# Rows of experts 2 to 6 turned by transposing transfers instead of by TensorE

## The chip, the cores and the metric

The kernel runs on one core of a Trainium2 chip. The core has five engines with queues of their own: TensorE (PE; PEld is its weight load), VectorE (DVE), ScalarE (ACT), GpSimd (POOL) and SyncE (SP), and 16 DMA engines that move what POOL, SP and ACT issue. The metric is device time in microseconds (us) of one execution, lower is better, given as the median of several runs.

## The reference

A chunked attention with memory (4 batches, 8 heads, 768 positions, head size 64) gives 3072 rows of 512 numbers. A noisy top-2 router sends each row to two of eight experts, and each expert is a two-layer product with a ReLU between:

```python
noisy_logits = logits + noise_scale * noise
top2 = np.argpartition(-noisy_logits, 2, axis=1)[:, :2]
...
for e in range(E):
    for k in range(2):
        mask = top2[:, k] == e
        h = np.maximum(x[mask] @ w1[e], 0.0)
        out[mask] += top2_w[mask, k, None] * (h @ w2[e])
```

Here `w1[e]` is 512 x 1024 and `w2[e]` is 1024 x 512. The change lies in the expert part alone.

## The kernel before

The first part (to about 110 us of the span) computes attention and router, and writes all rows with their eight gates to a table in device memory, `x_rows`. A row is 264 words: 512 bf16 numbers in 256 words, then 8 gates.

The second part works by *buckets*. Each pair of experts (28 pairs) has a bucket of up to 128 rows that chose both. `gather` (L693 to L699) fetches a bucket's rows by an indirect transfer on POOL's queue into one of eight `xl` buffers, row by partition. `turn` (L701 to L707) brings it into the form in which the first product reads it: four TensorE transposes of 128x128 into PSUM, one VectorE copy to the bucket's columns of `xTb`, and one ScalarE copy of the gates into `meta`. Rows over a bucket's limit take a side path (`spill`, `spart`) that the change does not touch.

Experts run one after the other (L877). For expert e, `first` (L758) multiplies `w1[e]` with the `xTb` columns of its seven buckets, in two groups (`big`, four buckets, 512 columns; `small`, three, 384 columns), each in eight `ps_h` groups of four matmuls, with four PSUM buffers; the ReLUs alternate between ScalarE (L754) and VectorE (L756). Then `second` (L777) does one bucket after another: eight matmuls into one of two `ps_y` buffers, drained with the gate as scale by ScalarE into an accumulator (the bucket's first expert) or by VectorE onto it (its second), after which POOL scatters the rows to the output (L788) and SP copies six rows to `spart` (L795).

A bucket is gathered and turned once, for the earlier of its two experts: `plan[e]` holds the new buckets of expert e, 7, 6, 5, 4, 3, 2, 1 and 0 of them. The order is written out by hand. After `first` of expert e the gathers of `plan[e + 1]` are issued, then the load of `w1[e + 2]`; after each bucket of `second` one of `plan[e + 1]` is turned; at the end `w2[e + 2]` is loaded. The weight loads, gathers and scatters are all on POOL's queue, in this order. SP has only the `spart` and `meta` transfers of the side path here.

Of the kernel before, what the change touches and what calls it, by code (L numbers as in the profile page):

```python
# [12 lines left out]
F32 = mybir.dt.float32  # L13
BF16 = mybir.dt.bfloat16
# [10 lines left out]
def kernel(  # L25
# [14 lines left out]
    nc = tc.nc  # L40
# [7 lines left out]
    E, F = moe_w1.shape[0], moe_w1.shape[2]  # L48
    KP = Dm // 128
# [19 lines left out]
    XC = Dm // 2  # L69
# [12 lines left out]
    def color(p):  # L82
        a, d = p % E, p // E + 1
        side = 0 if d == E // 2 else (a >> (1 if d == 2 else 0)) & 1
        return side * (E // 2) + d - 1
# [13 lines left out]
    def body():  # L99
# [63 lines left out]
        for hd in range(2 * GP):  # L163
            nc.sync.dma_start(
                out=mv_nat[QW * hd + WP:QW * hd + QW].rearrange("p g e d -> p g (e d)"),
                in_=bass.AP(mem_v.tensor, mem_v.offset + hd * n_mem * D, [[2 * D, n_mem // 2], [2 * GP * n_mem * D, NG], [1, 2 * D]]))
# [369 lines left out]
        def load_w1(e):  # L536
            w1t = w1bufs[e % 3]
            nc.gpsimd.dma_start(out=w1t, in_=moe_w1[e].rearrange("(kp p) f -> p kp f", p=128))
            W1[e] = w1t

        def load_w2(e):
            w2t = w2bufs[e % 3]
            nc.gpsimd.dma_start(out=w2t, in_=moe_w2[e].rearrange("(fb p) d -> p fb d", p=128))
            W2[e] = w2t
# [140 lines left out]
        xTv = xTb.rearrange("p k (g c) -> p k g c", c=CAP)  # L685
        meta = xg.tile([128, NB, E], F32, name="meta")
# [4 lines left out]
        got = {}  # L691

        def gather(p):  # L693
            idx = gidx if p in plan[0] else gidx2
            xl = ld.tile([128, ROW], I32, name="xl")
            nc.gpsimd.indirect_dma_start(  # L696
                out=xl, out_offset=None, in_=xd, in_offset=bass.IndirectOffsetOnAxis(ap=idx[:, p:p + 1], axis=0),
                bounds_check=N - 1, oob_is_err=True)
            got[p] = xl  # L699

        def turn(p, other=False):  # L701
            xl = got[p]
            p_t = psY.tile([128, KP, CAP], BF16, name="p_t2", tag="ps_y") if other else psX.tile([128, KP, CAP], BF16, name="p_t")
            for kp in range(KP):
                nc.tensor.transpose(out=p_t[:, kp, :], in_=xl[:, kp * 64:(kp + 1) * 64].bitcast(BF16), identity=identb)  # L705
            nc.vector.tensor_copy(xTv[:, :, p, :], p_t)  # L706
            nc.scalar.copy(meta[:, p, :], xl[:, XC:].bitcast(F32))  # L707

        def gather_spill(s_gi):
            xl = ld.tile([128, ROW], I32, name="xl")  # L710
            nc.gpsimd.indirect_dma_start(
                out=xl[:SPILL], out_offset=None, in_=xd, in_offset=bass.IndirectOffsetOnAxis(ap=s_gi[:, 0:1], axis=0),
                bounds_check=N - 1, oob_is_err=True)
            got["s"] = xl
# [17 lines left out]
        def halves(e):  # L732
            up = [(d - 1) * E + e for d in range(1, E // 2 + 1) if d < E // 2 or e < E // 2]
            dn = [(d - 1) * E + (e - d) % E for d in range(1, E // 2 + 1) if d < E // 2 or e >= E // 2]
            return sorted((sorted(up), sorted(dn)), key=lambda x: -len(x))
# [62 lines left out]
        plan = []  # L798
# [78 lines left out]
        for e in range(E):  # L877
            big, small = halves(e)
            if e == E - 1:
                end = nc.values_load(n_spill_i[0:1, 0:1], min_val=SPILL, max_val=N)  # L880
                past = xg.tile([128, NP], F32, name="past")
                nc.vector.tensor_scalar(out=past, in0=srank, scalar1=-float(SPILL), scalar2=None, op0=Alu.add)
            ht = hp_.tile([128, FB, (E - 1) * CAP], BF16, name="ht")
            if e == 0:
                parts = [big[:2], big[2:], small]
                off = 0
                for x, ps in enumerate(parts):
                    for j, p in enumerate(ps):
                        turn(p, j % 2 == 1)
                    if x == 2:  # L890
                        turn_spill()
                        find_tails()
                    first(W1[e], ht, off, ps, nc.scalar if x == 0 else None, CAP if x == 2 else OWN, big if x == 2 else ())
                    off += len(ps)
                    if x == 0:
                        s_gi, s_si = find_spill()
                        gather_spill(s_gi)
                        load_w2(1)
            else:
                first(W1[e], ht, 0, big)  # L900
                first(W1[e], ht, len(big), small)
            nxt = list(plan[e + 1]) if e + 1 < E else []
            for p in nxt:
                gather(p)
            if e + 2 < E:
                load_w1(e + 2)
            order = big + small

            for j, p in enumerate(order):
                second(e, p, ht, j, W2[e])  # L910
                if nxt:
                    turn(nxt.pop(0))
                if e == E - 1 and j == 1:
                    for x in range(1, E // 2 - 1):
                        nc.vector.tensor_tensor(out=spart[:, 0, :], in0=spart[:, 0, :], in1=spart[:, x, :], op=Alu.add)
            if e == E - 1:
                assert color(order[-1]) >= NCOL
                nc.vector.tensor_tensor(out=spart[:, 0, :], in0=spart[:, 0, :], in1=spart[:, E // 2 - 1, :], op=Alu.add)
                nc.gpsimd.indirect_dma_start(
                    out=out_part[NB], out_offset=bass.IndirectOffsetOnAxis(ap=s_si[:, 0:1], axis=0),  # L920
                    in_=spart[:, 0, :], in_offset=None, bounds_check=N - 1, oob_is_err=False)
            while nxt:
                turn(nxt.pop(0))
            if e + 2 < E:
                load_w2(e + 2)
        return end, past, ovc, ramp_i, onesb, identb, psX, psY, first, ld, hp_, xg, accs, load_w1, load_w2, W1, W2, relu, psH

    with tc.manual_schedule():
        kept = body()
# [3 lines left out]
    with tc.For_i(SPILL, end, 128) as i:  # L933
# [7 lines left out]
        for t in range(NP):  # L941
# [11 lines left out]
            out=xl, out_offset=None, in_=xd, in_offset=bass.IndirectOffsetOnAxis(ap=gi[:, 0:1], axis=0),  # L953
# [10 lines left out]
        with tc.For_i(0, E, 1) as e:  # L964
# [17 lines left out]
            out=out, out_offset=bass.IndirectOffsetOnAxis(ap=si[:, 0:1], axis=0),  # L982
            in_=o, in_offset=None, bounds_check=N - 1, oob_is_err=False)
# [30 lines left out]
```

## Time and profile before

| | |
|---|---|
| median of 3 runs | 337.96 us (335.78 to 338.23) |
| the profiled execution | 335.33 us, its span 333.7 us |
| mean granted clock of TensorE | 0.957 |
| TensorE (PE) busy | 288.1 us, 86% |
| DVE, ACT, POOL busy | 169.9, 133.4, 138.6 us |
| first product (L769) | 640 matmuls |
| second product (L780) | 448 matmuls |
| turns (L705) | 112 matmuls, 28 buckets |
| gathers (L696) | 28, median 6.5 us from issue to landing |

The profile is of one execution. A row of a group has line, engine, operation, tiles and shapes, then busy us, mean ns of one, and the idle time ahead of it with what ended it. Times in an order of time are us from the start of the span. Matmuls are pipelined, so the drawn lengths of neighbours overlap, and the distance between starts is what counts. L numbers are those of the kernel before, unless the kernel after is named.

### The profile page before, as it was taken

To read this page: it belongs to the slowest core of one execution; us is meant where nothing else is said; L and a number is where in the kernel's file an instruction comes from. 1 tells how busy PE (TensorE), PEld (TensorE's weight loads), DVE (VectorE), ACT (ScalarE), POOL (GpSimd) and SP (SyncE) were. 2 spreads that over 40 slices of the span, in tenths; PEclk is the share of its full clock that TensorE was granted. 3 is DMA by queue.
4 is the path that set the end of the run, shared out by engine and by line. 5 is a ranking of instruction groups with operands and counts; after the bars stand their busy time and mean duration, and the time that the engine had idled before them with its cause. 6 is when DMAs were issued, how large, how long until landed. Compare 5 with 4: busy or idle time off the path is not lost.

```text
span 333.7 us, 7301 instructions
## 1 busy us (share of the span) xinstructions
PE 288.1 (86%) x3019; PEld 173.5 (52%) x3019; DVE 169.9 (51%) x343; ACT 133.4 (40%) x235; POOL 138.6 (42%) x181
## 2 busy tenths in 40 slices
PE   1697887977776377999999999999999999999990
PEld 0575675755654256554754754544544544544540
DVE  7789859849958775222322323424342433434451
ACT  7877788757433033533333332332303303202200
POOL 7877868538023472781008007007152042042152
PEclk9999999979989559999999999999999999999997
DMA  7999999999997136699407905914959624521031
GB/s 99 179 163 176 184 163 163 210 143 101 214 225 216 23 88 93 128 156 238 87 0 125 221 4 110 223 28 105 207 147 166 117 111 70 86 109 60 1 140 71
DMA packets 58763, 42.99 MB, mean 129 GB/s; under 512 B 32449, under 2 KB 52033, under 8 KB 58728
## 3 DMA queue, kind: packets, MB, share of 16 engines
q0 software_dynamic: 49808, 38.71, 77.0%
q1 hardware_dynamic: 8632, 3.74, 5.6%
q8 instruction: 24, 0.39, 0.5%
q10 hardware_dynamic: 288, 0.07, 0.1%
q14 instruction: 11, 0.09, 0.1%
HBM read 61.23 MB, written 10.66 MB: 215 GB/s over the span
## 4 chain that ended last, share of the span: by engine, by line
PE 43%; issue 24%; DVE 13%; ACT 8%; POOL 7%; DMA 3%; POOLq 0%; DVEq 0%; ACTq 0%
PE ps_h L769 16%; PE ps_y L780 14%; POOL out_dram L788 4%; ACT kd L276 3%; PE ps_o L345 3%; DMA out_dram<-acc,sidx 2%; PE ps_o L341 2%; DVE mx L313 2%; DVE xrow L358 2%; DVE sd L318 2%; DVE vg L150 2%; PE p_t L705 2%; ACT xt L371 1%; ACT P L320 1%; PE p_t L265 1%
## 5 line engine op out<-in xcount | busy, mean ns | idle before, releaser
L769 PE MATMUL ps_h<-xTb,w1t 128*128 128x512 bf16 (+5 forms) x640 | 101.4, 320 | 1.5 <-DVE xTb L706 1.5
L780 PE MATMUL ps_y<-w2t,ht 128*128 128x512 bf16 x448 | 101.4, 379 | 0.0
L769 PEld LDWEIGHTS <-w1t 128*128 128x128 bf16 x640 | 58.6, 99 | 43.9 <-DVE xTb L706 1.1
L788 POOL DMA_INDIRECT out_dram<-acc,sidx x28 | 28.1, 1004 | 126.4 <-DVE acc L787 124.1
L756 DVE TENSOR_SCALAR ht<-ps_h 128x512 bf16<-128x512 f32 (+3 forms) x68 | 38.1, 560 | 68.1 <-PE ps_h L769 63.1
L780 PEld LDWEIGHTS <-ht 128*128 128x128 bf16 x448 | 42.9, 98 | 46.7
L754 ACT ACTIVATE ht<-ps_h 128x384 bf16<-128x384 f32 (+2 forms) x76 | 38.9, 511 | 70.4 <-PE ps_h L769 66.3
L784 ACT ACTIVATE acc<-ps_y,meta 128x512 f32<-128x512 f32 x28 | 19.2, 687 | 62.6 <-PE ps_y L780 45.4
L787 DVE SCALAR_TENSOR_TENSOR acc<-ps_y,meta,acc 128x512 f32<-128x512 f32 x28 | 21.0, 750 | 34.5 <-PE ps_y L780 34.5
L696 POOL DMA_INDIRECT xl<-x_rows,gidx x28 | 30.0, 1071 | 16.8 <-PE ps_h L769 6.6
L134 POOL DMA_DIRECT2D vg<-in_v_dram x34 | 25.5, 756 | 11.4 <-DMA kg<-in_k_dram 3.7
L706 DVE COPY xTb<-p_t 128x512 bf16<-128x512 bf16 x28 | 11.6, 422 | 28.6 <-PE p_t L705 28.4
L276 ACT COPY kd<-p_t 64x768 bf16<-64x768 bf16 x32 | 25.2, 786 | 1.0 <-PE p_t L265 0.8
L265 PE MATMUL p_t<-identb,qg 128*64 128x128 bf16 x192 | 10.3, 245 | 12.0 <-DMA qg<-in_q_dram 6.6
L371 ACT COPY xt<-p_x 128x768 bf16<-128x768 bf16 x16 | 12.8, 798 | 12.0 <-PE p_x L369 11.9
L341 PE MATMUL ps_o<-memv,PT 128*128 128x260 bf16 x96 | 15.0, 296 | 2.2 <-DVE PT L332 2.0
L320 ACT ACTIVATE P<-sd 128x768 bf16<-128x768 f32 x16 | 13.5, 845 | 8.1 <-DVE sd L318 8.1
L268 ACT COPY qT<-p_t 128x768 bf16<-128x768 bf16 x16 | 12.8, 800 | 8.9 <-PE p_t L265 8.8
L358 DVE TENSOR_TENSOR xrow<-ps_o,rec 128x768 bf16<-128x768 f32 x16 | 15.3, 958 | 0.6
L313 DVE TENSOR_REDUCE mx<-ps_s 128x12 f32<-128x768 f32 x16 | 15.1, 942 | 0.5 <-PE ps_s L300 0.5
L318 DVE TENSOR_TENSOR sd<-ps_s,mx 128x768 f32<-128x768 f32 x16 | 15.2, 949 | 0.0
L345 PE MATMUL ps_o<-vg,PT 128*32 128x256 bf16 x384 | 14.9, 293 | 0.0
(150 smaller groups left out, 287.5 us busy)
## 6 DMA issues: line engine op xcount, KB each, us to landing
w1t<-in_moe_w_dram POOLq DMA_DIRECT2D x8, 1024.0 KB, 11.4
w2t<-in_moe_w_dram POOLq DMA_DIRECT2D x8, 1024.0 KB, 10.1
vg<-in_v_dram POOLq DMA_DIRECT2D x30, 168.0 KB, 10.2
qg<-in_q_dram POOLq DMA_DIRECT2D x7, 384.0 KB, 9.9
kg<-in_k_dram POOLq DMA_DIRECT2D x7, 384.0 KB, 11.3
x_rows<-xrow SPq DMA_DIRECT2D x3, 792.0 KB
x_rows<-xrow SPq DMA_DIRECT2D x2, 384.0 KB
xl<-x_rows,gidx POOLq DMA_INDIRECT x28, 6.5
```

The lines of the kernel that those rows point to most:

```text
L134: nc.gpsimd.dma_start(out=vg[p0 + j:p0 + j + nj, c:c + n, hd, :, :].rearrange("p c e d -> p c (e d)"), in_=bass.AP(v.tensor, v.offset + (g ...
L276: nc.scalar.copy(st[n]["kT"][hs, hh, :].rearrange("d (p j) -> d p j", j=SJ), st[n]["p_k"][hs].rearrange("d j p -> d p j"))
L313: nc.vector.tensor_reduce(out=mx, in_=st[n]["ps"], axis=AX, op=Alu.max)
L318: nc.vector.tensor_tensor(out=sd, in0=st[n]["ps"], in1=bc4(st[n]["mx"], CTX), op=Alu.subtract)
L345: nc.tensor.matmul(out=po[32 * r:32 * r + 32, u, :MD], lhsT=PT[:, 2 * u + e, 32 * r:32 * r + 32], rhs=vg[:, CB * half + x, :, e, :], start ...
L358: nc.vector.tensor_tensor(out=xr.rearrange("p u (h d) -> p u h d", d=D), in0=po[:, :, :MD].rearrange("p u (h d) -> p u h d", d=D), in1=rec ...
L696: nc.gpsimd.indirect_dma_start(out=xl, out_offset=None, in_=xd, in_offset=bass.IndirectOffsetOnAxis(ap=idx[:, p:p + 1], axis=0), bounds_ch ...
L754: nc.scalar.activation(out=dst, in_=src, func=Act.Relu)
L756: nc.vector.tensor_scalar(out=dst, in0=src, scalar1=0.0, scalar2=None, op0=Alu.max)
L769: nc.tensor.matmul(out=ps_h[:, o:o + w], lhsT=w1t[:, kp, f * 128:(f + 1) * 128], rhs=rhs(kp), start=(kp == 0 and i == 0), stop=(kp == KP - ...
L780: nc.tensor.matmul(out=ps_y, lhsT=ht[:, f, j * CAP:(j + 1) * CAP], rhs=w2t[:, f, :], start=(f == 0), stop=(f == FB - 1))
L788: nc.gpsimd.indirect_dma_start(out=out_part[p], out_offset=bass.IndirectOffsetOnAxis(ap=sidx[:, p:p + 1], axis=0), in_=a, in_offset=None, ...
```

## The change

For the buckets of experts 2 to 6 (15 of the 28) a new function, `turn_far`, takes the place of `turn`: it gathers the bucket and then issues four transposing transfers on SP's queue, from the gathered rows straight to the bucket's columns of `xTb`. They are issued during expert e for expert e + 2. The seven buckets of expert 0 and the six of expert 1 are turned by TensorE as before, and the gates of the fifteen are copied by ScalarE all together, at the end of expert e.

```diff
+        def turn_far(p):
+            gather(p)
+            for kp in range(KP):
+                nc.sync.dma_start_transpose(out=xTv[:, kp, p, :], in_=got[p][:, kp * 64:(kp + 1) * 64].bitcast(BF16))
+
...
-            nxt = list(plan[e + 1]) if e + 1 < E else []
+            nxt = list(plan[1]) if e == 0 else []
             for p in nxt:
                 gather(p)
+            far = list(plan[e + 2]) if e + 2 < E else []
             if e + 2 < E:
                 load_w1(e + 2)
+            if e == 0:
+                for p in far[:2]:
+                    turn_far(p)
             order = big + small
 
             for j, p in enumerate(order):
                 second(e, p, ht, j, W2[e])
                 if nxt:
                     turn(nxt.pop(0))
+                late = j + 2 if e == 0 else j
+                if late < len(far):
+                    turn_far(far[late])
...
-            while nxt:
-                turn(nxt.pop(0))
+            for p in far:
+                nc.scalar.copy(meta[:, p, :], got[p][:, XC:].bitcast(F32))
             if e + 2 < E:
                 load_w2(e + 2)
```

How it moves instructions is seen at three places. On TensorE, between the first and the second bucket of expert 1's second product; `ps_y` is a bucket's sum, `xl` a gathered bucket. Before, the last matmul of one bucket, a turn, and the first of the next:

```order
L780 MATMUL ps_y_3322<-w2t1_2645,ht_3172 128x512
L705 LDWEIGHTS xl_3301
L705 MATMUL p_t_3332<-identb_93,xl_3301 128x128
L705 LDWEIGHTS xl_3301
L705 MATMUL p_t_3332<-identb_93,xl_3301 128x128
L705 LDWEIGHTS xl_3301
L705 MATMUL p_t_3332<-identb_93,xl_3301 128x128
L705 LDWEIGHTS xl_3301
L705 MATMUL p_t_3332<-identb_93,xl_3301 128x128
L780 LDWEIGHTS ht_3172
L780 MATMUL ps_y_3339<-w2t1_2645,ht_3172 128x512
```

After, at the same place:

```order
L785 LDWEIGHTS ht_3217
L785 MATMUL ps_y_3347<-w2t1_2645,ht_3217 128x512
L785 LDWEIGHTS ht_3217
L785 MATMUL ps_y_3365<-w2t1_2645,ht_3217 128x512
L785 LDWEIGHTS ht_3217
```

The eight rows of the turn are gone, and the next bucket follows at once.

On POOL, in expert 0, from the last gather for expert 1 to the first scatter of expert 1. Before:

```order
L696 DMA xl_3054<-x_rows,gidx2_2716 128x264
L538 DMA w1t2_2644<-in_moe_w1_dram 128x4x1024
L543 DMA w2t2_2646<-in_moe_w2_dram 128x8x512
L696 DMA xl_3301<-x_rows,gidx2_2716 128x264
L696 DMA xl_3305<-x_rows,gidx2_2716 128x264
L696 DMA xl_3309<-x_rows,gidx2_2716 128x264
L696 DMA xl_3313<-x_rows,gidx2_2716 128x264
L696 DMA xl_3317<-x_rows,gidx2_2716 128x264
L538 DMA w1t0_162<-in_moe_w1_dram 128x4x1024
L788 DMA out_0_dram<-acc0_2650,sidx_2620 3072x512
```

After:

```order
L696 DMA xl_3054<-x_rows,gidx2_2716 128x264
L538 DMA w1t2_2644<-in_moe_w1_dram 128x4x1024
L696 DMA xl_3059<-x_rows,gidx2_2716 128x264
L696 DMA xl_3067<-x_rows,gidx2_2716 128x264
L696 DMA xl_3092<-x_rows,gidx2_2716 128x264
L696 DMA xl_3117<-x_rows,gidx2_2716 128x264
L696 DMA xl_3142<-x_rows,gidx2_2716 128x264
L543 DMA w2t2_2646<-in_moe_w2_dram 128x8x512
L538 DMA w1t0_162<-in_moe_w1_dram 128x4x1024
L696 DMA xl_3357<-x_rows,gidx2_2716 128x264
```

The five gathers of expert 2 stand ahead of the load of `w2[2]` instead of behind it, and the four of expert 3 (the first is the last row) come right behind the load of `w1[3]`, ahead of expert 1's scatter. SP issues four transposing transfers for each of these gathers, 20 and then 16, ahead of its first `spart` transfer.

On ScalarE, at the end of expert 0. Before, a gate copy stood behind the drain of a bucket, and the ReLUs of expert 1 (`ht`) followed the last drain:

```order
L784 ACTIVATE acc5_2655<-ps_y_3144,meta_2648 128x512
L707 COPY meta_2648<-xl_3054 128x8
L784 ACTIVATE acc6_2656<-ps_y_3161,meta_2648 128x512
L754 ACTIVATE ht_3172<-ps_h_3173 128x512
L754 ACTIVATE ht_3172<-ps_h_3185 128x512
```

After:

```order
L789 ACTIVATE acc6_2656<-ps_y_3201,meta_2648 128x512
L935 COPY meta_2648<-xl_3059 128x8
L935 COPY meta_2648<-xl_3067 128x8
L935 COPY meta_2648<-xl_3092 128x8
L935 COPY meta_2648<-xl_3117 128x8
L935 COPY meta_2648<-xl_3142 128x8
L759 ACTIVATE ht_3217<-ps_h_3218 128x512
```

Five gate copies of expert 2's buckets, each waiting for its gather, now stand between expert 0's last drain and expert 1's first ReLU.

## The prediction

> **What bounds the kernel now.** I read the busy shares first, then the table of windows, then the order of time on TensorE.
>
> ```profile
> PE 288.1 (86%) x3019; PEld 173.5 (52%) x3019; DVE 169.9 (51%) x343; ACT 133.4 (40%) x235; POOL 138.6 (42%) x181
> 150.00:160.00 10.00, 10.00 (x56) 4.96 (x55) 3.00 (x5) 3.85 (x7) 1.26 (x2) 1.00 1.16 233
> 180.00:200.00 20.00, 20.00 (x146) 12.09 (x145) 6.64 (x13) 6.84 (x15) 2.96 (x4) 1.00 0.66 127
> 240.00:260.00 20.00, 20.00 (x101) 9.38 (x100) 6.74 (x11) 4.84 (x9) 6.91 (x7) 1.00 0.82 165
> ```
>
> A window row gives its bounds and length, then busy time of PE, PEld, DVE, ACT and POOL, the granted clock, the DMA share and GB/s. In the expert stage TensorE is busy for the whole of each window at a granted clock of 1.00, while DVE and ACT are busy for about a third. The other engines wait for TensorE there:
>
> ```profile
> DVE ht L756 <- PE ps_h L769: 60.7, 56, 6.2
> ACT ht L754 <- PE ps_h L769: 59.3, 59, 5.3
> DVE acc L787 <- PE ps_y L780: 34.5, 27, 4.4
> ```
>
> (What waited, for whom, us in total, times, longest; from 133 to 326 us.) So in this stage only two things count: what TensorE issues, and whether anything makes it stop. Its order of time shows both, here for expert 1's second product and the starts of the next experts:
>
> ```profile
> 150.66 1.89 PE L780 MATMUL ps_y<-w2t,ht 128*128 128x512 bf16 x8
> 152.39 12.35 PE L769 MATMUL ps_h<-xTb,w1t 128*128 128x512 bf16 x96
> ...
> 170.43 1.89 PE L780 MATMUL ps_y<-w2t,ht 128*128 128x512 bf16 x8
> 172.15 0.39 PE L705 MATMUL p_t<-identb,xl 128*128 128x128 bf16 x4
> 172.38 1.89 PE L780 MATMUL ps_y<-w2t,ht 128*128 128x512 bf16 x8
> 174.10 0.39 PE L705 MATMUL p_t<-identb,xl 128*128 128x128 bf16 x4
> 174.33 3.62 PE L780 MATMUL ps_y<-w2t,ht 128*128 128x512 bf16 x16
> 177.78 12.35 PE L769 MATMUL ps_h<-xTb,w1t 128*128 128x512 bf16 x96
> 189.97 1.89 PE L780 MATMUL ps_y<-w2t,ht 128*128 128x512 bf16 x8
> ...
> 202.95 12.27 PE L769 MATMUL ps_h<-xTb,w1t 128*128 128x512 bf16 x64
> ```
>
> The first number is the start. Starts are to be subtracted, not lengths, because the pipelined ends overlap. A bucket with a turn takes 174.33 - 172.38 = 1.95 us, one without takes (177.78 - 174.33) / 2 = 1.725 us. **A turn is worth 0.225 us of TensorE**, though its four instructions are drawn 0.39 us long.
>
> **What goes.** Fifteen buckets (5, 4, 3, 2, 1 for experts 2 to 6) are no longer turned by TensorE: 15 x 0.225 = 3.4 us, all of it on the path. The thirteen turns of experts 0 and 1 stay, with their places. The copies from PSUM go with them:
>
> ```profile
> L706 DVE COPY xTb<-p_t 128x512 bf16<-128x512 bf16 x28 | 11.6, 422 | 28.6 <-PE p_t L705 28.4
> ```
>
> 15 x 0.42 = 6.3 us of VectorE, worth nothing, since VectorE waits for TensorE. The faster cadence needs no cover that is not there: pairs and longer runs of buckets without a turn already keep 1.725 us, so the two PSUM buffers of `ps_y` and their drain are not the next limit. After the last expert the scatters follow TensorE's last bucket, and move with it.
>
> **What is added: 60 transposing transfers on SP.** No row of before shows one. The nearest rows are SP's plain transfers (min/median/max ns) and its queue (packets, MB, share of the 16 engines):
>
> ```profile
> L548 SPq DMA_DIRECT2D x_rows<-xrow x6: 359/362/371, 58.8 to 111.2; - x6
> L215 SPq DMA_DIRECT2D nz_all<-in_moe_noise_dram x4: 665/1344/2292, 6.5 to 60.2; - x4
> L730 SPq DMA_DIRECT2D meta<-xl x6: 670/671/830, 128.8 to 132.8; - x6
> q1 hardware_dynamic: 8632, 3.74, 5.6%
> ```
>
> Let T be the pace of a stream of such transfers. Lower end: SP's shortest row, 0.36 us. For the upper end, a packet costs 5.6% x 333.7 x 16 / 8632 = 35 ns of one DMA engine; if a 128x128 block is written in pieces of 16 source rows, 32 bytes for each of 128 partitions, that is 1024 writes, 64 for each of 16 engines, T = 2.2 us (the longest SP row, 2.29 us, says the same). I take 0.67 us, the row of the transfers from SBUF to SBUF, nearest in kind. The program gives this queue eight completion counters, so up to eight transfers can be in flight, and the time to land sets the pace only if it is over 8 x 0.67 = 5.4 us.
>
> The transfers cost nothing if they are done before TensorE asks. The gathers set the start. The rows of POOL and the times from issue to landing of before:
>
> ```profile
> 141.94 0.83 POOL L538 DMA_DIRECT2D w1t<-in_moe_w_dram  x1
> 142.74 0.97 POOL L543 DMA_DIRECT2D w2t<-in_moe_w_dram  x1
> 144.01 1.11 POOL L696 DMA_INDIRECT xl<-x_rows,gidx  x1 [0.30 <-ACT meta L707]
> 149.42 1.01 POOL L696 DMA_INDIRECT xl<-x_rows,gidx  x1 [0.30 <-issue]
> ...
> w2t<-in_moe_w_dram POOLq DMA_DIRECT2D x1, 1024.0 KB, 13.1
> xl<-x_rows,gidx POOLq DMA_INDIRECT x1, 12.2
> xl<-x_rows,gidx POOLq DMA_INDIRECT x1, 8.3
> w2t<-in_moe_w_dram POOLq DMA_DIRECT2D x1, 1024.0 KB, 10.0
> xl<-x_rows,gidx POOLq DMA_INDIRECT x2, 2.9
> ```
>
> The landing rows are, in order: the `w2t` load issued at 142.74, the gathers issued at 144.01 and 149.42, a lone load at 176.43, and two gathers near 135 with nothing ahead. The five gathers landed from 156.2 to 157.7, right behind the load ahead of them (142.74 + 13.1 = 155.8): this queue delivers in order, and a lone load takes 10 us. The change puts `load_w2(2)` behind the gathers, so only `w1t` is ahead: it lands near 142 + 10 = 152, and the five gathers from 152.2 to about 153.6. The first transfer starts at about 152.2.
>
> Deadlines, from the starts above less the turns saved: expert 2's first product at 177.78 - 5 x 0.225 = 176.7, whose first four buckets need 16 transfers; expert 3's at 202.95 - 9 x 0.225 = 200.9, by when 20 + 16 = 36 must be done. That allows (176.7 - 152.2) / 16 = 1.53 us and (200.9 - 152.2) / 36 = **1.35 us each**; later experts ask for 12, 8 and 4 in 24 us each, so the second one decides. At T = 0.67 the 36 are 24 us of work in 49 us. No stall, and the sum stands.
>
> The Trainium skill speaks against the change: VectorE: DVE Perf Modes, The three transpose paths, has 390 ns for a 128x128 bf16 block on TensorE and 1309 ns by the DMA crossbar, and advises TensorE where PSUM will do as the destination. This case's row has 0.225 us for four blocks in stream, so the first figure is no price here; by 1309 ns, if it were the pace, 36 would take 47.1 us and end at 199.3, still in time, and the sum would be the same.
>
> **What is moved.** `load_w2(2)` goes from 142.74 to about 149.5 and lands by 163 at 13.1 us; its first reader is at 189.97. The gathers of experts 3 to 6 now stand behind their expert's loads and some scatters, but are needed a whole expert (24 us) later. SP's `spart` transfers come behind the transfers that were issued earlier:
>
> ```profile
> 175.15 0.67 SPq L795 DMA_DIRECT2D spart<-acc  x1
> ```
>
> The first of them waits for the 36 only if T > (175.15 - 152.2) / 36 = 0.64 us, so by a us or two; it is waited for when its accumulator is used again, by expert 3 near 223.
>
> The `meta` copies of a whole expert now stand in one row on ScalarE, ahead of the next expert's ReLUs, and wait for gathers:
>
> ```profile
> 152.65 0.69 ACT L784 ACTIVATE acc<-ps_y,meta 128x512 f32<-128x512 f32 x1 [1.19 <-PE ps_y L780]
> 153.45 0.60 ACT L754 ACTIVATE ht<-ps_h 128x512 bf16<-128x512 f32 x1
> 155.18 0.60 ACT L754 ACTIVATE ht<-ps_h 128x512 bf16<-128x512 f32 x1 [1.13 <-PE ps_h L769]
> L707 ACT COPY meta<-xl 128x8 f32<-128x8 f32 x28 | 4.9, 191 | 10.9 <-DMA xl<-x_rows,gidx 10.8
> ```
>
> After expert 0 five copies, 5 x 0.19 = 1 us, come between 153.3 and the first ReLU. TensorE fills one of four `ps_h` buffers in (155.18 - 153.45) / 2 = 0.865 us and asks for the first again at 152.39 + 4 x 0.865 = 155.85. ScalarE must start that ReLU by 155.25; with the gathers there by 153.6 it starts at about 154.4. Cover: 0.8 us. Later experts' gathers land long before.
>
> **Sum.** The profiled execution took 335.33 us: 333.7 of span and 1.6 around it. 335.33 - 3.4 = 331.9. The median of the runs shown is 337.96, 2.6 above that execution; on its scale **334.6 us**.
>
> **Rivals.**
>
> *The transfers are the new bound.* If T is over 1.35 us, TensorE waits for `xTb` at the first products of experts 2 and 3. Against before, expert 3 then starts at 152.2 + 36 T instead of 202.95, and six later turns still save 1.35 us: at T = 1.8 it starts at 217.0, 12.7 us net lost, 350.7 us; at 2.2 us, 231.4, 27.1 lost, 365 us. For it: no row shows a transposing transfer, and the weight loads fill the DMA engines when the first ones run (share 1.16 from 150 to 160). Against: two of three SP rows are half of 1.35 us or less. This ends slower.
>
> *ScalarE's copies wait for late gathers.* If the last of expert 0's five gathers lands as late as before, at 157.7, the copy ends at 157.9, TensorE has stopped at 155.85 and goes on at about 157.9 + 0.6 = 158.5: 2.65 us lost, 0.7 us gained in all, 337.2. Pace between 1.35 and 1.45 us gives the same kind of result. Against: the order of loads on POOL, above.
>
> **How the numbers follow.** Free transfers 0.54; late copies or a pace just past the bound 0.12; transfers as the bound 0.34. A saving of 3.4 us is 1.0% of 337.96, and 1% is about what a measurement of this kernel can tell from no change (the runs shown spread over 0.7%). So the first case is split, 0.28 to faster and 0.26 to within 1%; the second gives 0.10 to within and 0.02 to faster; the third is slower. The range goes from 331.5, just under the 331.9 of the profiled execution, to 351, half way into the third case, by which about 0.17 lies above and 0.03 below. The likeliest case's own range is 331.5 to 336.
>
> **What would show it.** Right: a turnless bucket of 1.73 us in experts 1 to 5, first products starting near 176.7 and 200.9, no idle TensorE from 133 to the end, SP's transfers at under 1.35 us each, ScalarE's first ReLU of expert 1 by 155. Wrong: idle time of TensorE ahead of the first product of expert 2 or 3 with a transfer as its releaser, or ahead of expert 1's fifth `ps_h` with ScalarE as its releaser; or a slower cadence of the matmuls themselves while transfers run, which I hold at nothing because weight loads beside them leave it at 1.725 us.

## The result, and the profile after

The changed kernel takes 334.14 us against 336.96 us (medians of runs on the same chip; 332.74 to 339.32 and 335.78 to 338.23). The ratio is **0.9898, with a 95% interval from 0.9864 to 0.9933**: about 1% faster. Ratios here and below leave out slow executions and are not the plain quotient of the medians, which is 0.992 here. The forecast was 334.6 us and 0.990. The profiled execution took 333.82 us, its span 331.9 us; before these were 335.33 and 333.7.

So the span fell by 1.8 us, not by 3.4. Where the rest is, the order of time on TensorE tells. After the change its line numbers are L774 for the first product, L785 for the second. Here is the changed kernel from expert 0 on (start, length, engine, line, output and inputs, count, idle time ahead with its releaser):

```profile
129.46 6.17 PE L774 MATMUL ps_h<-xTb,w1t 128*128 128x384 bf16 x64
135.48 1.48 PE L785 MATMUL ps_y<-w2t,ht 128*128 128x512 bf16 x6
138.75 0.39 PE L785 MATMUL ps_y<-w2t,ht 128*128 128x512 bf16 x1 [1.79 <-DVE ht L761]
140.21 0.39 PE L785 MATMUL ps_y<-w2t,ht 128*128 128x512 bf16 x1 [1.07 <-DVE ht L761]
...
140.66 3.22 PE L785 MATMUL ps_y<-w2t,ht 128*128 128x512 bf16 x8
...
153.82 12.35 PE L774 MATMUL ps_h<-xTb,w1t 128*128 128x512 bf16 x96
166.00 12.25 PE L785 MATMUL ps_y<-w2t,ht 128*128 128x512 bf16 x56
178.09 12.35 PE L774 MATMUL ps_h<-xTb,w1t 128*128 128x512 bf16 x96
...
202.37 12.27 PE L774 MATMUL ps_h<-xTb,w1t 128*128 128x512 bf16 x64
...
299.14 12.27 PE L774 MATMUL ps_h<-xTb,w1t 128*128 128x512 bf16 x64
```

And of before, the last batch of expert 0's first product, and the first product of expert 7 (that of expert 1, at 152.39, stands in the prediction):

```profile
132.95 6.16 PE L769 MATMUL ps_h<-xTb,w1t 128*128 128x384 bf16 x64
...
301.06 9.18 PE L769 MATMUL ps_h<-xTb,w1t 128*128 128x512 bf16 x45
```

**The measure for all that follows** is the time from the start of expert 1's first product to the start of expert 7's. The fifteen removed turns all lie in it, and TensorE's granted clock is 1.00 in it unless something makes TensorE stop. Before it is 301.06 - 152.39 = 148.67 us, after it is 299.14 - 153.82 = **145.32 us: 3.35 us less**, where 15 x 0.225 = 3.375 was forecast. There is no idle time of TensorE in it.

The profiled execution kept only 1.8 of that because it lost time ahead of it. In expert 0 the ReLUs came late, TensorE stood idle twice (1.79 and 1.07 us), and then eight matmuls are drawn 3.22 us long instead of 1.89. The table of windows (bounds, length, busy time of PE, PEld, DVE, ACT and POOL, granted clock, DMA share, GB/s) names the second loss:

```profile
140.00:142.00 2.00, 1.79 (x10) 0.87 (x11) 0.52 (x2) 0.77 (x2) 1.67 (x2) 0.77 0.88 118
142.00:144.00 2.00, 2.00 (x9) 0.90 (x8) 0.06 (x1) 0.03 (x1) 1.01 (x1) 0.50 1.06 190
```

The clock was halved for about 3 us after the idle time; from 132 to 140 us, while the ReLUs came late, it was 1.00. From the last batch of expert 0's first product to expert 1's this execution took 153.82 - 129.46 = 24.4 us, and before 152.39 - 132.95 = 19.4. That is 4.9 us lost, while the stages ahead of 129 us were 3.5 us quicker. Both lie ahead of the first transposing transfer (148.2). The same slow stretch turns up below in a kernel without any such transfer, and is absent in other executions of the changed kernel, so the transfers don't make it; what first slows the ReLUs is not in the trace.

The transfers by the group of line 712 (min/median/max ns, first and last start):

```profile
L712 SPq DMA_TRANSPOSE xTb<-xl x60: 1093/1230/3244, 148.2 to 249.7; - x60
```

The same in SP's order of time, up to the transfers for expert 4:

```profile
148.20 50.21 SPq L712 DMA_TRANSPOSE xTb<-xl  x36
198.51 0.74 SPq L800 DMA_DIRECT2D spart<-acc  x1
199.36 17.51 SPq L712 DMA_TRANSPOSE xTb<-xl  x12
```

A transfer holds SP for 1.23 us, nearly twice the 0.67 taken; 36 of them took 50.21 us, 1.39 each. They end at 198.4, and expert 3 begins at 202.4: hidden, but with 4 us left in 54. This margin, not the sum, is what the experiments are about. ScalarE's order of time at the end of expert 0:

```profile
154.66 0.58 ACT L935 COPY meta<-xl 128x8 f32<-128x8 f32 x5
155.15 0.59 ACT L759 ACTIVATE ht<-ps_h 128x512 bf16<-128x512 f32 x1
```

The five gate copies found their gathers there and took 0.58 us together; the first ReLU of expert 1 starts at 155.15. What the turn took besides is gone as forecast: the copies from PSUM are 13 instead of 28, in the groups of the page:

```profile
L706 DVE COPY xTb<-p_t 128x512 bf16<-128x512 bf16 x13 | 5.3, 420 | 12.5 <-PE p_t L705 10.9 <-issue 1.5
```

### The profile page after: what moved, and what is told of

The parts are those of the page before. It is cut to its first block, busy times and chain, and to the rows that moved or that the text cites. A ratio compares the mean times of both kernels' runs of the same rounds, so it can differ in the third digit from the quotient of the medians.

```text
span 331.9 us, 7265 instructions
## 1 busy us (share of the span) xinstructions
PE 284.0 (86%) x2959; PEld 169.0 (51%) x2959; DVE 163.6 (49%) x328; ACT 133.1 (40%) x235; POOL 138.4 (42%) x181
## 3 DMA queue, kind: packets, MB, share of 16 engines
q1 hardware_dynamic: 18232, 5.71, 10.2%
## 4 chain that ended last, share of the span: by engine, by line
issue 36%; PE 18%; DMA 13%; POOL 9%; SPq 8%; DVE 7%; ACT 6%; another core or an unknown queue 1%; POOLq 1%; DVEq 0%
SPq L712 8%; POOL out_dram L793 5%; PE ps_h L774 5%; DMA kg<-in_k_dram 4%; PE ps_o L345 3%; PE ps_o L341 3%; DMA xl<-x_rows,gidx 3%; DMA out_dram<-acc,sidx 2%; DMA wgn_f<-in_moe_w_noise_dram 2%; ACT xt L371 2%; DVE xrow L358 1%; POOL xl L696 1%; ACT qT L268 1%; PE p_t L265 1%; ACT kd L276 1%
## 5 line engine op out<-in xcount | busy, mean ns | idle before, releaser
L785 PE MATMUL ps_y<-w2t,ht 128*128 128x512 bf16 x448 | 100.9, 383 | 2.9 <-DVE ht L761 2.9
L774 PE MATMUL ps_h<-xTb,w1t 128*128 128x512 bf16 (+5 forms) x640 | 101.2, 319 | 1.5 <-DVE xTb L706 1.5
L774 PEld LDWEIGHTS <-w1t 128*128 128x128 bf16 x640 | 58.5, 99 | 43.8 <-DVE xTb L706 1.1
L785 PEld LDWEIGHTS <-ht 128*128 128x128 bf16 x448 | 43.8, 99 | 54.5 <-DVE ht L761 3.8
L134 POOL DMA_DIRECT2D vg<-in_v_dram x34 | 25.4, 751 | 8.4 <-PE ps_s L305 3.5
L320 ACT ACTIVATE P<-sd 128x768 bf16<-128x768 f32 x16 | 13.5, 845 | 6.8 <-DVE sd L318 6.8
L341 PE MATMUL ps_o<-memv,PT 128*128 128x260 bf16 x96 | 14.1, 284 | 1.9 <-DVE PT L332 1.8
L265 PEld LDWEIGHTS <-qg 128*64 128x64 bf16 x192 | 7.3, 123 | 12.6 <-DMA qg<-in_q_dram 6.8
```

What stands on the lines that cost most here:

```text
L134: nc.gpsimd.dma_start(out=vg[p0 + j:p0 + j + nj, c:c + n, hd, :, :].rearrange("p c e d -> p c (e d)"), in_=bass.AP(v.tensor, v.offset + (g ...
L341: nc.tensor.matmul(out=po[:, u, :OW], lhsT=PT[:, 2 * u + e, :], rhs=memv[:, g, e, :], start=(e == 0), stop=False, skip_group_check=True)
L774: nc.tensor.matmul(out=ps_h[:, o:o + w], lhsT=w1t[:, kp, f * 128:(f + 1) * 128], rhs=rhs(kp), start=(kp == 0 and i == 0), stop=(kp == KP - ...
L785: nc.tensor.matmul(out=ps_y, lhsT=ht[:, f, j * CAP:(j + 1) * CAP], rhs=w2t[:, f, :], start=(f == 0), stop=(f == FB - 1))
```

## The experiments

The theory: the gain is TensorE's fifteen turns, and the transfers cost nothing as long as they land in time. The rivals: the gain comes from gathering an expert ahead, or the transfers do cost something that the profiled execution happens not to show. The kernels ran in three groups, each beside its own runs of the kernel before (medians 333.1, 338.57 and 332.96 us), the first two on one chip and the third on another; ratios are within a group.

### The same kernel again: the cover is thin

> The changed kernel once more, on the chip of the runs beside it. Theory (fifteen turns of 0.225 us leave TensorE, the transfers are hidden): 3.4 us less than before, ratio 0.990, and again 157.4 us from the start of expert 1's first product to the start of expert 7's second. The 2.9 us that TensorE idled in expert 0's second product in the profiled execution come from a stretch at half clock that lies elsewhere in each execution, so here they stand at another place or are smaller. Rival (the change itself makes that stall): the same idle time at the same place, before the first transposing transfer.

The changed kernel, run again, took 331.39 us against 333.1, ratio 0.9948 (0.9910 to 0.9986), where 0.990 was expected. Expert 0 has no such idle time here, so the change does not make it each time. The half clock, which the expectation took for its cause, came behind the idle time in the first trace, not ahead of it. But the order of time on TensorE has waits that the first trace has not:

```profile
151.21 12.35 PE L774 MATMUL ps_h<-xTb,w1t 128*128 128x512 bf16 x96
...
175.48 7.51 PE L774 MATMUL ps_h<-xTb,w1t 128*128 128x512 bf16 x37
183.42 0.33 PE L774 MATMUL ps_h<-xTb,w1t 128*128 128x128 bf16 x2 [0.43 <-DMA xTb<-xl]
185.68 4.84 PE L774 MATMUL ps_h<-xTb,w1t 128*128 128x128 bf16 x57 [1.93 <-DMA xTb<-xl]
...
299.21 12.27 PE L774 MATMUL ps_h<-xTb,w1t 128*128 128x512 bf16 x64
```

299.21 - 151.21 = 148.00: of the 3.35 us only 0.67 is left in this execution. TensorE has done the four buckets of expert 2 that go together and waits for the fifth, whose transfers are number 17 to 20. The group of line 712 up to there:

```profile
L712 SPq DMA_TRANSPOSE xTb<-xl x20: 1095/1230/2197, 150.1 to 178.0; - x20
```

And the window of the wait:

```profile
180.00:185.00 5.00, 3.31 (x19) 1.63 (x18) 1.38 (x2) 1.19 (x2) 0.21 (x1) 1.00 1.31 169
```

SP began the twentieth at 178.0, in good time for 183.0; what it writes was there at 185.68, 7.7 us later. The DMA engines are full at this point: their share is 1.31 between 180 and 185. What runs there are the next two weight loads, issued on POOL at 174.35 and 175.30. So a transfer's time on SP is not its time to land. The trace also holds the signals by which the transfers report that they have landed, which the views don't print: numbers 13 to 17 landed 2.3 to 3.0 us after SP began them, numbers 18 to 20 after 6.7 to 7.6 (the twentieth at 185.64).

> The changed kernel a third time, beside the two below. Theory (its fifth bucket for expert 2 lands between just in time and some 2.7 us late, execution by execution): 145.3 to 148.0 us from expert 1's to expert 7's first product, ratio between 0.990 and 0.995. Rival (the one late execution seen was an accident): 145.3 us, ratio 0.990.

Once more, in another group: 330.93 against 332.96, ratio 0.9932 (0.9895 to 0.9970). TensorE's order of time has two waits:

```profile
182.04 4.84 PE L774 MATMUL ps_h<-xTb,w1t 128*128 128x128 bf16 x57 [0.57 <-DMA xTb<-xl]
220.54 3.61 PE L785 MATMUL ps_y<-w2t,ht 128*128 128x512 bf16 x16 [0.60 <-ACT acc L789]
```

ScalarE's has one just ahead of the second, and the weight loads of TensorE (PEld) have one at expert 3's first product:

```profile
219.80 0.69 ACT L789 ACTIVATE acc<-ps_y,meta 128x512 f32<-128x512 f32 x1 [2.54 <-DMA spart<-acc]
199.66 11.25 PEld L774 LDWEIGHTS <-w1t 128*128 128x128 bf16 x61 [0.55 <-DMA xTb<-xl]
```

The measure is 296.57 - 149.52 = 147.05, 1.73 us over 145.32. Two losses make it: from expert 1 to expert 3 it takes 198.80 - 149.52 = 49.28 instead of 202.37 - 153.82 = 48.55 (0.73, the fifth bucket again), and from expert 3 to expert 4 it takes 223.99 - 198.80 = 25.19 instead of 24.19 (1.00). Of the second, 0.24 us are lost in expert 3's first product (12.34 us to the start of the second product instead of 12.10), where the fourth matmul waits for the last of the 36 transfers. The other 0.76 us are a queue effect: a `spart` transfer stood on SP behind the twelve transfers for expert 4, ScalarE waited 2.54 us for it before it could use the accumulator, and TensorE then found no free `ps_y`. In the first two traces ScalarE waited for a `spart` transfer too, 1.6 and 1.1 us, but TensorE did not stop.

Why did the first trace show neither? From the first transfer to where TensorE asks for the end of the fifth bucket (about 7.5 us into expert 2) there are 178.09 + 7.5 - 148.2 = 37.4 us there, and 175.48 + 7.5 - 150.1 = 32.9 and 173.79 + 7.67 - 148.5 = 33.0 in the other two. The needed time, first transfer to the twentieth's landing, was 35.6 and 33.5 us in these two. The slow stretch of expert 0 lengthened the time that covered the transfers: the first one began 5.6 us ahead of expert 1's first product there, and 1.1 and 1.0 us ahead of it in the other two. It also put the next weight loads later. Their first, in the three traces in turn:

```profile
176.96 0.99 POOL L543 DMA_DIRECT2D w2t<-in_moe_w_dram  x1
174.35 0.99 POOL L543 DMA_DIRECT2D w2t<-in_moe_w_dram  x1
172.66 0.98 POOL L543 DMA_DIRECT2D w2t<-in_moe_w_dram  x1
```

In the first trace SP had begun the twentieth transfer at 175.1, ahead of these loads, and it landed 2.4 us later; in the others it began at 178.0 and 174.6, behind them, and landed after 7.6 and 7.4 us. **That the profiled execution shows no wait is luck**, not margin.

### One transfer for a bucket

```diff
-            for kp in range(KP):
-                nc.sync.dma_start_transpose(out=xTv[:, kp, p, :], in_=got[p][:, kp * 64:(kp + 1) * 64].bitcast(BF16))
+            nc.sync.dma_start_transpose(out=xTv[:, :, p, :], in_=got[p][:, :XC].bitcast(BF16))
```

> One transposing transfer of 128x512 for each far bucket in place of four of 128x128. Theory (transfers hidden, so their pace does not matter under about 1.5 us for 128x128): the time of the changed kernel within 0.3%, ratio 0.990. SP's rows say what sets the pace: if each instruction costs SP a fixed time, 1.2 to 1.5 us for a bucket instead of 4.9; if each block of 16 rows costs it, again about 4 to 5 us.

329.1 us against 333.1, ratio 0.9900 (0.9856 to 0.9944).

Its transfers as a group, and its order of time on TensorE:

```profile
L711 SPq DMA_TRANSPOSE xTb<-xl x15: 1190/1217/5163, 152.7 to 244.1; - x15
```

```profile
151.94 12.35 PE L773 MATMUL ps_h<-xTb,w1t 128*128 128x512 bf16 x96
...
297.26 12.27 PE L773 MATMUL ps_h<-xTb,w1t 128*128 128x512 bf16 x64
```

An instruction that turns all four blocks holds SP for 1.22 us at the median, as long as one that turns a single block; beside the weight loads up to 5.16 us. Nine of them, for experts 2 and 3, kept SP for 21.1 us where 36 kept it for 50; they were done on SP at 173.8, ahead of the next weight loads at 175.08, and by its signal the fifth bucket's transfer landed at 171.9, near 12 us before TensorE asked for it (176.22 + 7.5 = 183.7). The measure is 145.32, although this execution has no slow stretch: the whole gain, without luck.

> One transfer of 128x512 for a far bucket, again. Theory (never late, so the whole 3.4 us): 145.3 us from expert 1's to expert 7's first product and ratio 0.990; not above that of the changed kernel beside it.

In the third group 329.22 against 332.96, ratio 0.9919 (0.9886 to 0.9951), again 145.32 (294.02 - 148.70) and no wait. In both groups its median is below that of the changed kernel beside it (329.1 to 331.39, 329.22 to 330.93). It is the fastest complete form in both. The intervals overlap (0.9856 to 0.9944 beside 0.9910 to 0.9986 in the first group), so the sign rests on both groups agreeing and on the waits that are gone from the trace.

### No turn at all: how much the turns are worth

```diff
-            for kp in range(KP):
-                nc.sync.dma_start_transpose(out=xTv[:, kp, p, :], in_=got[p][:, kp * 64:(kp + 1) * 64].bitcast(BF16))
...
-                first(W1[e], ht, 0, big)
-                first(W1[e], ht, len(big), small)
+                stand = halves(0)[0] if e >= 2 else None
+                first(W1[e], ht, 0, big, stand=stand)
+                first(W1[e], ht, len(big), small, stand=stand)
```

This kernel gathers the rows of experts 2 to 6 but doesn't turn them; the first products of experts 2 to 7 read columns of expert 0 in their place.

> Left out: the buckets of experts 2 to 6 are not turned at all, neither by TensorE nor by transfers; the first products of experts 2 to 7 read expert 0's columns in their place, in the same shapes. Theory: the transfers cost nothing where they are, so this takes the time of the changed kernel within 0.3% (ratio to before 0.990). Rival (the transfers slow the weight loads, the gathers or TensorE's reads): faster than the changed kernel by what they cost, 1 us or more.

330.01 us against 333.1, ratio 0.9906 (0.9863 to 0.9948); measure 295.19 - 149.87 = 145.32. Not turning at all is worth no more than one transfer for a bucket (0.9900). So transfers that land in time cost nothing that these runs can tell (their intervals reach 0.4% to each side), in contention neither, and 3.35 us is all that this change can bring in these stages.

### The gathers ahead, all turns on TensorE

```diff
-            nxt = list(plan[1]) if e == 0 else []
-            for p in nxt:
+            nxt = list(plan[e + 1]) if e + 1 < E else []
+            for p in nxt if e == 0 else ():
                 gather(p)
...
-            for kp in range(KP):
-                nc.sync.dma_start_transpose(out=xTv[:, kp, p, :], in_=got[p][:, kp * 64:(kp + 1) * 64].bitcast(BF16))
...
-            for p in far:
-                nc.scalar.copy(meta[:, p, :], got[p][:, XC:].bitcast(F32))
```

> One part alone: the gathers an expert ahead, in the changed kernel's order on POOL, but all turns by TensorE as before, no transposing transfers. Theory (the gain is the fifteen turns that leave TensorE): the time of before, ratio 1.000, and 1.95 us for a bucket with a turn. Rival (the earlier gathers are worth something, or the moved load of expert 2's second weights costs something): off by 0.3% or more.

340.87 us against 338.57, ratio 1.0020 (0.9976 to 1.0064): no difference that can be told. The measure is 308.52 - 159.85 = 148.67, exactly that of before. Gathering ahead does not bring the 1% by itself. Its trace also has the slow stretch, with no transposing transfer in the whole program:

```profile
143.62 0.39 PE L783 MATMUL ps_y<-w2t,ht 128*128 128x512 bf16 x1 [2.55 <-DVE ht L759]
...
159.85 12.35 PE L772 MATMUL ps_h<-xTb,w1t 128*128 128x512 bf16 x96
...
308.52 12.27 PE L772 MATMUL ps_h<-xTb,w1t 128*128 128x512 bf16 x64
```

From the last batch of expert 0's first product (132.75) to 159.85 it took 27.1 us. All traces of this second group show idle time of that kind in expert 0; none of those of the first and third do. The kernel before was 5.5 us slower in this group than in the first, on the same chip, so it may meet the stretch too, but it was not traced there: that the early gathers have a part in the stretch is not excluded.

### More transfers: where the bound lies

Each bucket's first transfer is issued a second time:

```diff
-            for kp in range(KP):
+            for kp in (0, 1, 2, 3, 0, 1, 2, 3)[:KP + 1]:
```

> The first of each far bucket's four transfers issued a second time. Theory (a queue at 1.4 to 1.5 us each): the twenty of expert 2's first four buckets end near 178 to 180 against a first product at 175, the next five near 185 to 188, the twenty more for expert 3 near 213 to 217 against 202, so 11 to 15 us more than the changed kernel, 342 to 348 on this chip. Rival (only single late transfers cost): 2 to 4 us more.

356.06 us in one run, against a median of 338.57 for the kernel before in its group; 342 to 348 was expected. SP's order of time, then TensorE's, then two windows:

```profile
149.90 66.87 SPq L712 DMA_TRANSPOSE xTb<-xl  x45
```

```profile
192.56 6.70 PE L774 MATMUL ps_h<-xTb,w1t 128*128 128x128 bf16 x63 [3.29 <-DMA xTb<-xl]
223.38 13.61 PE L774 MATMUL ps_h<-xTb,w1t 128*128 128x512 bf16 x64 [12.04 <-DMA spart<-acc]
```

```profile
215.00:220.00 5.00, 0.00 (x0) 0.00 (x0) 0.00 (x0) 0.00 (x0) 1.06 (x1) 0.59 1.28 149
220.00:225.00 5.00, 1.61 (x4) 0.58 (x5) 0.00 (x0) 0.00 (x0) 0.00 (x0) 0.50 1.20 191
```

A quarter more transfers, and the queue is the bound: 45 take 66.87 us, 1.49 each. TensorE waits 3.29 us at expert 2's fifth bucket and 12.04 at expert 3. (The releaser named at 223.38 is the `spart` transfer that stands right behind the last transposing one on SP.) The miss has two parts. The last transfer left SP at 149.90 + 66.87 = 216.8, but the product began at 223.4, 6.6 us later, beside weight loads issued at 211.70 and 212.64 that filled the DMA engines (share 1.28, 1.20). And after the idle time the clock was down to 0.50, so the next matmuls ran at half pace: the measure is 321.50 - 157.82 = 163.68, 18.36 over 145.32, of which 15.33 are the waits; the other 3 are put down to the clock, which was at 0.50 after both waits (192 to 194 and 220 to 225).

All four a second time:

```diff
-            for kp in range(KP):
+            for kp in (0, 1, 2, 3, 0, 1, 2, 3)[:KP + 4]:
```

> Each of the four transfers of a far bucket issued twice. Theory (SP's queue takes 1.2 to 1.4 us for each, one after the other): 72 of them are due before expert 3's first product and take 88 to 101 us from 148, so that product starts at 236 to 249 instead of 202, and the kernel takes 34 to 47 us more, about 368 to 381. Rival (they overlap, and SP's row is only the time that it is held in a queue that has room): no wait of TensorE, 334.

401.84 us in one run, against a median of 333.1; 368 to 381 was expected. SP's order of time, TensorE's, and a row of the table of waits (who waited for what, us in total, times, longest):

```profile
147.88 106.57 SPq L712 DMA_TRANSPOSE xTb<-xl  x72
```

```profile
194.55 1.01 PE L774 MATMUL ps_h<-xTb,w1t 128*128 128x512 bf16 x2 [21.03 <-DMA xTb<-xl]
251.87 0.59 PE L774 MATMUL ps_h<-xTb,w1t 128*128 128x512 bf16 x1 [27.25 <-DMA xTb<-xl]
289.17 5.59 PE L785 MATMUL ps_y<-w2t,ht 128*128 128x512 bf16 x15 [11.60 <-ACT acc L789]
```

```profile
ACT acc L789 <- DMA spart<-acc: 13.5, 1, 13.5
```

The pace is the same, 106.57 / 72 = 1.48 us (1.2 to 1.4 was expected), and expert 3's first product starts at 251.87, as the last of its transfers leave SP (147.88 + 106.57 = 254.45). What the expectation missed is the third wait: ScalarE waited 13.5 us for a `spart` transfer that stood behind transposing ones on SP, and TensorE lost 11.60 us by it. The third run of the changed kernel shows the same effect in small. The rest is small waits between single matmuls and the halved clock behind each pause (0.59 us for one matmul in the rows above).

### Loads later

In expert 1 the loads of `w2[2]` and `w1[3]` are issued after the four gathers of expert 3 and not ahead of them:

```diff
-            if e + 2 < E:
+            if e + 2 < E and e != 1:
                 load_w1(e + 2)
...
+                if e == 1 and j == 3:
+                    load_w2(2)
+                    load_w1(3)
...
-            if e + 2 < E:
+            if 0 < e < E - 2:
                 load_w2(e + 2)
```

> The changed kernel with the loads of expert 2's second and expert 3's first weights issued behind the gathers of expert 3 (near 160 us instead of 148). Theory (four transfers for a bucket are late for expert 2's fifth bucket in some executions, because the weight loads slow the first twenty transfers): those end by about 177 instead of 181 to 186, no wait in expert 2, ratio 0.990 as with one transfer for a bucket. Rival (SP's own 1.23 us for each is the whole of it): the twentieth ends at the same time, the wait in expert 2 stays, ratio 0.995.

336.92 us against 338.57, ratio 0.9929 (0.9892 to 0.9967), measure 304.68 - 159.36 = 145.32, no wait.

```profile
L712 SPq DMA_TRANSPOSE xTb<-xl x20: 1172/1230/2021, 151.7 to 177.1; - x20
```

The twenty took 25.4 us from the first start to the last, against 26.9, 27.9 and 26.1 in the three traces of the changed kernel. But this execution had the slow stretch, by which the small group of expert 2 asked only at 183.64 + 7.5 = 191.1, so its missing wait proves nothing. Also, the loads beside the twentieth transfer in the repeats are the next two, issued near 174, which this kernel leaves where they are. What the loads do is seen in the landing signals: the moved ones were issued at 161.68 and 162.62, and of the transfers begun before that those whose signals the trace holds landed after 2.3 to 3.0 us, while numbers 9 to 16, begun behind, took 6.7 to 9.5. On SP all took 1.23 us at the median, as before. So the loads slow the landing; whether moving them helps the kernel **stays open**.

### Expert 1 too

One transfer for a bucket, for expert 1's six buckets as well:

```diff
             for p in nxt:
-                gather(p)
+                turn_far(p)
...
                 if nxt:
-                    turn(nxt.pop(0))
+                    p1 = nxt.pop(0)
+                    nc.scalar.copy(meta[:, p1, :], got[p1][:, XC:].bitcast(F32))
```

> One transfer of 128x512 for a far bucket, and the six buckets of expert 1 turned by such transfers too. Theory (0.225 us of TensorE for each turn, and the six transfers from about 137 us done before expert 1's first product near 150): six more turns saved, 21 x 0.225 = 4.7 us less than before, ratio 0.986. Rival (there is too little time for expert 1's transfers behind the gathers and beside the weight loads): TensorE waits at expert 1's first product, ratio 0.990 or above.

336.06 us against 338.57, ratio 0.9912 (0.9877 to 0.9946), where 0.986 was expected. The six turns more were worth 6 x 0.225 = 1.35 us by the theory, and nothing of it shows beside the 0.9900 and 0.9919 of the form with one transfer for a bucket. The trace has the slow stretch in expert 0, which hides the reason. The same kernel in the third group:

> The same with expert 1's six buckets turned by such transfers too, again, beside the kernel with one transfer for a far bucket. Theory: 1.35 us less than that kernel, 0.4%, ratio about 0.986; seen in the trace as 1.725 us for each bucket of expert 0 where the clock is full. Rival (expert 1's six transfers give back what they save, by late gate copies or a wait at expert 1's first product): the same time as that kernel or more.

333.54 us against 332.96, ratio 0.9979 (0.9943 to 1.0014): the gain cannot be told from none. The profiled execution (334.81 us, 1.3 above this median) shows where it can go. ScalarE's order of time:

```profile
150.77 0.20 ACT L935 COPY meta<-xl 128x8 f32<-128x8 f32 x1 [2.28 <-DMA xl<-x_rows,gidx]
...
156.18 0.20 ACT L935 COPY meta<-xl 128x8 f32<-128x8 f32 x1 [3.34 <-DMA xl<-x_rows,gidx]
```

then TensorE's, and a window ahead of it:

```profile
148.03 3.61 PE L773 MATMUL ps_h<-xTb,w1t 128*128 128x512 bf16 x16 [0.32 <-DMA xTb<-xl]
156.92 10.54 PE L773 MATMUL ps_h<-xTb,w1t 128*128 128x512 bf16 x80 [5.28 <-ACT ht L758]
```

```profile
140.00:146.00 6.00, 6.00 (x29) 2.73 (x28) 0.00 (x0) 2.32 (x6) 4.78 (x6) 1.00 1.19 108
```

The gathers for expert 2 were issued from 139.6 to 144.9, as in the kernel with one transfer for a bucket beside it (139.4 to 144.7), but six transfers of four blocks more ran with them, at a DMA share of 1.19 (1.07 there, same window), and they landed later: the last of ScalarE's five gate copies begins at 156.18, against 149.9 there. TensorE, with all `ps_h` buffers full, loses 5.28 us at expert 1's fifth `ps_h` group. The measure is 300.43 - 148.03 = 152.40, 7.1 us over 145.32. That is more than the kernel loses as a rule, since its median is 4.3 us above that of the form beside it. The wait is that of the prediction's second rival, in a kernel that has no slack left for it; that the six transfers are what delays the gathers is argued from these times, not shown by a run of its own.

## Why the prediction was right, and where it was not

**The sum: right.** 15 x 0.225 = 3.375 us were forecast; 3.35 went, in five traces with transposing transfers alike to a hundredth (all that have 145.32), and the kernel with no turns in experts 2 to 6 has the same. The seconds keep their cadence: 56 matmuls in 12.25 us without a turn between. In the ratio, 334.6 / 337.96 = 0.990 was forecast and 0.9898 measured. The repeats, 0.9948 and 0.9932, lie lower in gain, though the intervals of all three overlap; their traces say why, below.

**The pace of the transfers, T: wrong.** The step took 0.67 us from the nearest kind of row. Measured: 1.23 us at the median on SP, 1.39 for each of 36 with the waits, 1.48 and 1.49 in the longer streams. The choice of row failed: SP's plain transfers from SBUF to SBUF are no measure for a transposing one. The upper end's 1024 writes for a block were not it either: queue q1 has 18232 - 8632 = 9600 packets more on the page after, 160 for each transfer. 1.39 is past the 1.35 named as the bound. That TensorE still did not wait is owed to the slow stretch, which put expert 3 later and allowed (202.37 - 148.2) / 36 = 1.50 us. Without it, and without losses ahead (expert 3 at 48.55 us after expert 1's start), the two repeats would have allowed (199.76 - 150.07) / 36 = 1.38 and (198.07 - 148.48) / 36 = 1.38, against paces of 1.40 and 1.38.

The Trainium skill's figure (VectorE: DVE Perf Modes, The three transpose paths: 1309 ns for a 128x128 bf16 block by the DMA crossbar) was the better guide to T, 6% over the measured 1.23 us. Its cost by block does not carry over to one transfer of four blocks, which held SP no longer (1.22 us at the median).

**The deadlines: one too few, and for the wrong event.** The step asked when SP would be done with the first 16 and the first 36. The fifth bucket of expert 2 (numbers 17 to 20, asked for 7.5 us after expert 2 begins) was left out. And it counted to the end on SP, where what counts is the landing: up to 7.7 us after the twentieth began, with weight loads beside it. This is the deadline that failed in both repeats, by 2.4 and 0.6 us. Expert 3, which the prediction called the one that decides, was hardly safer. In the first trace the 36th transfer left SP at 198.4, 4 us ahead of it. In the second it left at 200.6, in time for 202.44 only because expert 2's wait had moved expert 3 from 199.76. In the third it left at 198.0 for 198.80 and landed at 199.62, and the product lost 0.24 us.

**`spart` behind the transfers: held, but not harmless.** The prediction looked at the first one only. A later one, behind the twelve transfers for expert 4, cost TensorE 0.76 us in the third run and 11.60 with the doubled transfers.

**ScalarE's gate copies: right.** The first ReLU of expert 1 was to start near 154.4 and by 155.25 at the latest; it started at 155.15, behind a TensorE that was itself 1.4 us later (153.82 against 152.39), with no wait. The five copies took 0.58 us together where 1 us was taken. In the form that moves expert 1's turns as well this wait does come.

**The rivals.** "The transfers are the new bound" did not come true as priced (350 us and more), but its mechanism did: in two of three traces of the changed kernel the transfers, by late landings and a late `spart`, take back 1.7 and 2.7 of the 3.35 us, and a quarter more of them makes it 356 us. A chance of 0.34 for it was fair; the 0.54 for transfers that are free came out, in the execution that was traced, by a cover that a slow expert 0 had lengthened: luck, by the repeats. That the slower cadence of matmuls beside transfers is nothing held: 145.32 with and without them.

**What stays open:** why expert 0 is slow in some executions, and whether another place for the weight loads would make the kernel faster.

## What to carry to other kernels

Work that moves from a full engine to a queue is free only up to its landing, so list every consumer's deadline, the small last group's too, and price the landing beside the loads that run then. Whatever stood on that queue before is now behind the new work, so ask for each such transfer who waits for it. And when one instruction can move four blocks, compare it with four: here it takes the same time on the queue as one, and it turned a margin near zero into a safe one (0.9900 and 0.9919, against 0.9948 and 0.9932 for the four-transfer form beside it, which had 0.9898 in its first runs).

## What was not expected of the hardware

- A transposing transfer of 128x128 holds SP for 1.23 us at the median (1.09 to 3.24), one of 128x512 for 1.22 (up to 5.16, beside weight loads, and 6.70 in the second run).
- A transposing transfer of 128x128 landed 2.3 to 3.0 us after its start where no weight load ran with it and up to 12.0 us after it where one did (the changed kernel's second run), while its time on SP stayed 1.23 us at the median. Up to 7.7 us went by between a start on SP and the use, at a DMA share of 1.31.
- After about 12 us without work TensorE ran at a granted clock of 0.50 (windows 215 to 225 of the kernel with a quarter more transfers), and after two pauses, 2.9 us together, it did so as well (142 to 144 us of the changed kernel), so a wait can cost more than its own length. Waits of 0.43 and 1.93 us in the changed kernel's second run left it at 1.00. The Trainium skill (TensorE: Matmul & The Clock Gate, Part 1: The HAM clock gate) states half the clock after an idle window of about 3.4 us; the 0.50 after the 12 us agrees, while each of the two short pauses is below that.
